# Pooled attention and a maxout layer on one core: weight casts as one-element reductions, a weight difference on GpSimd, another order of the first loads

## The chip, the cores and the metric

The kernel runs on one core of a Trainium2 chip. A core has five engines with a queue of their own each: TensorE (PE, matrix products; its weight loads are shown as PEld), VectorE (DVE), ScalarE (ACT), GpSimd (POOL) and SyncE (SP), which in this kernel only issues DMAs. Each engine takes its instructions strictly in the order of its queue and waits on semaphores for the others. The metric is the device time of one execution in microseconds (us); less is better.

## The reference

For 8 batches and 8 heads, with S = 1152 positions and head size D = 64, queries are averaged in pairs, attention is taken over all keys, and the result goes, all heads side by side, through a layer that takes the greater of two projections.

```
q_pool = q.reshape(B, H, S // 2, 2, D).mean(axis=3)          # 576 queries a head
attn   = softmax(q_pool @ k^T / sqrt(D))
x      = (attn @ v), heads side by side                      # 4608 tokens x 512
out    = maximum(x @ w1, x @ w2) @ w_out                     # 512 -> 1024 -> 512
```

All inputs and the output are float32 in HBM; the kernel works in bfloat16 with float32 accumulation.

## The kernel before

**The mathematics used.** maximum(h1, h2) is computed as relu(h1 - h2) + h2. So the kernel makes three things of the weights once, at the start: `wd` = w1 - w2 (bf16, 512 x 1024), `wo` = w_out in bf16, and `w21` = w2 @ w_out (512 x 512). A block of tokens then needs h = relu(x @ wd), and out = h @ wo + x @ w21.

**Weights.** Each of w1, w2 and w_out is loaded in four tiles of 512 KB (`w_load`, by part 0 = w2, 1 = w1, 2 = w_out, and tile 0 to 3). On landing, `w_cast` (L597) puts one VectorE instruction per tile in the queue: a copy to bf16 for w2 (L599, into `w2b`) and w_out (L606, into `wo`), a subtraction for w1 (L602, into `wd`). All are 128 partitions x 1024 elements, f32 in SBUF to bf16 in SBUF. `w2t_job` transposes w2 on TensorE (L614, copied out at L620), and when all tiles of w2 and w_out are cast, `w21_jobs` puts 32 products of 512 columns each (L630, copied out at L635) into TensorE's pool of filler work. These f32 tiles live in space that later holds other data: w2 in columns of `xT`, w1 where the hidden layer `gT` will be.

**Attention.** Two heads of a batch make a pair; there are 32, four to a batch. For each pair q, k and v come in one DMA of 576 KB each (`load_q`, `load_k`, `load_v`), into three buffers in turn. GpSimd makes bf16 of them: q with the sum of neighbours in two halves (`cast_q`, L319, 64 partitions x 576), k in L284, v in L326. For pairs 0 and 1 the sum for q is on VectorE (`cast_q0`, L310). q and k are transposed on TensorE for pairs 0 to 4 (L345, L361, L388, copied out by VectorE at L352, L368, L395) and by DMA after that (L302, L375). Scores (L510) are made in 324 groups of 512 columns for two heads into a ring of three PSUM buffers; ScalarE exponentiates each group (L517). A pair has 10.125 groups. The product with v (L420, and L432 for the last 64 rows) is divided by its sum on VectorE (`norm`: L442, L447, L452, into `xnat`). When the four pairs of a batch are done, its tokens are transposed into `xT` (L572 and L578 for the first and last batch, DMA for the others).

**Layer.** Blocks of 512 tokens: `h_pairs` (L699, copied out at L708) and `p_pair` (L732, copied out at L744), and, once all scores are issued, the single forms `h_jobs` (L672) and `p_job` (L767).

**Order of the work.** No order is written by hand except at the start. A planner (`class Plan`) runs while the program is built: it keeps an assumed time for each engine, with an assumed cost for each instruction, and the main loop picks at each step what TensorE does next: a group of scores, or one unit of a job (transposes, products with v, w21, layer). Jobs sit in two lanes, and more once the layer begins. Everything on the other engines is put in their queues as those picks bring it about. So an assumed cost changes the order of all that follows. `flush` runs ahead of each step; it hands DMAs from a list named `line` to SP, in the order of the list, when the assumed DMA backlog is under 4 us and the buffer is free; it emits the casts of a pair that has landed (`casts`); and it takes one weight cast from `lazy` when VectorE is assumed free and no transpose of q or k is near. The cast of the weights has no due time:

```
if lazy and plan.free.get("DVE", 0.0) <= now() and not any(
        queue[kind] and ready_at(queue[kind][0]) <= now() + 1.5 for kind in "qk") and all(
        j is None or j.kind not in "qk" for j in lane.values()):
    lazy.pop(0)()
```

**The start** (L1110 to L1150) is a list: q0 in two parts around k0, then loads that are issued at once (`load_q(1)`, `got_w((0, 0))`) and loads that go to `line` (`load('w', (0, 2), got_w, 'w2f2')`). `cast_v(0)` is put in GpSimd's queue there as well. In `got_w((part, tile))`, part and tile are as in `w_load`. Before the change the order is: q0 (first part), k0, q0 (rest), q1, k1, w2 tiles 0 and 1, v0, w2 tile 3; by `line` then w2 tile 2, q2, k2, w_out tiles 3, 1, 2, k3, v1, w_out tile 0, q3, w1 tiles 0 and 3, k4, w1 tile 2, v2, q4, w1 tile 1, v3. Later loads are appended to `line` as buffers come free.

**Who waits for wd.** `more_moe` opens a block of the hidden layer only when all tiles of `wd` are in the plan, and each unit of L699 names the tile `wd{ct}` that it reads.

Of the kernel before, what the change touches and what calls it, by code (L numbers as in the profile page):

```python
# [10 lines left out]
RELU = mybir.ActivationFunctionType.Relu  # L11
COPY = mybir.ActivationFunctionType.Copy
ALU = mybir.AluOpType


class Plan:
# [144 lines left out]
def bass_funnel_attn__then__act_maxout2_kernel(  # L161
# [10 lines left out]
    C, F = moe_w1.shape  # L172
# [21 lines left out]
    with ctx:  # L194
# [401 lines left out]

        def w_cast(part, ct):  # L597
            if part == 0:
                dve(lambda e: e.tensor_copy(w2b[:, ct, :], w2f[:, ct, :]),  # L599
                    [f"w2f{ct}"], [f"w2b{ct}"], 0.69)  # L600
            elif part == 1:
                dve(lambda e: e.tensor_tensor(  # L602
                    wd[:, ct, :], w1f[:, ct, :], w2f[:, ct, :], ALU.subtract),
                    [f"w1f{ct}", f"w2f{ct}"], [f"wd{ct}"], 1.4)
            else:
                dve(lambda e: e.tensor_copy(  # L606
                    wo[:, 2 * ct:2 * ct + 2, :], wof[:, 2 * ct:2 * ct + 2, :]),
                    [f"wof{ct}"], [f"wo{2 * ct}", f"wo{2 * ct + 1}"], 0.69)

        def w2t_job(ct):  # L610
            def go(e, m):
# [52 lines left out]
        def h_jobs(nb, tail):  # L664
            n0, n1 = hblocks[nb]
            size = n1 - n0
            g0 = n0 % RING
            jobs = []
            for ft in range(NF):
                def part(ct, ft=ft):  # L670
                    def go(e, m):
                        return e.matmul(fb[m][:, 0:size], wd[:, ct, ft * P:(ft + 1) * P],  # L672
                                        xT[:, ct, n0:n1], start=(ct == 0), stop=(ct == NC_ - 1))
                    return unit([f"wd{ct}"] + xkeys(n0, n1), 0.216 * size / 512, go)

# [12 lines left out]

        def h_pairs(nb):
            n0, n1 = hblocks[nb]  # L690
            size = n1 - n0
            g0 = n0 % RING
            jobs = []
            for f0 in range(0, NF, 2):
                def part(ct, turn, f0=f0):
                    def pair(e, m):
                        for k in range(2):
                            z = rows(turn ^ k)
                            last = e.matmul(  # L699
                                fb[m + k][:, 0:size], wd[z, ct, (f0 + k) * P:(f0 + k + 1) * P],  # L700
                                xT[z, ct, n0:n1], start=(turn == 0 and ct == 0),
                                stop=(turn == 1 and ct == NC_ - 1))
                        return last
                    return duo([f"wd{ct}"] + xkeys(n0, n1), 0.217 * size / 512, pair, turn == 1 and ct == 0)

                def evac(m, f0=f0):
                    w = [f"gT.{g}.{f0 + k}" for k in range(2) for g in gkeys(n0, n1)]
                    dve(lambda e: e.tensor_scalar_max(  # L708
                        gT[:, f0:f0 + 2, g0:g0 + size], wide[m // 2][:, :, 0:size], 0.0),
                        [f"f{m}", f"f{m + 1}"], w + [f"f{m}", f"f{m + 1}"], 0.16 + 2 * size / 960.0)  # L710
                jobs.append(Job("h", [part(ct, turn) for turn in range(2) for ct in range(NC_)],
                                evac, nb=nb, single=lambda f0=f0: h_jobs(nb, True)[f0:f0 + 2]))
            return jobs
# [114 lines left out]
        loaded = {}  # L828
        casts = []
        lazy = []  # L830
        todo = []
        MARGIN = 0.6
        K_PE = (0, 1, 2, 3, 4)
# [47 lines left out]
        def got_w(at):  # L881
            n, ct = at
            w_load(n, ct)

            def ready():
                w_cast(n, ct)
                if n == 0:
                    queue["w"].append(w2t_job(ct))
                w_done.add((n, ct))
                if n != 1 and all((m, c) in w_done for m in (0, 2) for c in range(NC_)):  # L890
                    queue["w"].extend(w21_jobs())
            later(f"{('w2f', 'w1f', 'wof')[n]}{ct}", lambda: lazy.append(ready))

        def enter(i):
            if i + 2 < NPAIR:
# [13 lines left out]
        def flush():  # L909
            for entry in list(todo):  # L910
                if plan.ops[entry[0]]["seen"] + entry[3] <= now():
                    todo.remove(entry)
                    entry[1]()
            while line and plan.dma_free - now() < DEPTH and plan.when("SP", w=[line[0][3]]) <= now() + 0.6:
                kind, i, fn, key = line.pop(0)
                fn(i)
                loaded[kind, i] = len(plan.ops) - 1
            for kind, i in list(casts):
                if not landed(kind, i):
                    continue  # L920
                if kind == "k":
                    force(("k", i - 2))
                    if k_hi.get(i - 2) != NT:
                        continue
                casts.remove((kind, i))
                {"k": start_k, "q": start_q, "v": start_v}[kind](i)
            if lazy and plan.free.get("DVE", 0.0) <= now() and not any(
                    queue[kind] and ready_at(queue[kind][0]) <= now() + 1.5 for kind in "qk") and all(
                    j is None or j.kind not in "qk" for j in lane.values()):
                lazy.pop(0)()  # L930
            for o in list(held):
                if plan.ops[plan.writer[f"osb{o}"]]["seen"] + 2.0 <= now():
# [32 lines left out]
        def more_moe():  # L965
            tail = nxt == NGR
            step = P if tail else 2 * P
            while h_at[0] < len(hblocks):
                n0, n1 = hblocks[h_at[0]]
                keys = xkeys(n0, n1) + [f"wd{ct}" for ct in range(NC_)]  # L970
# [149 lines left out]
        queue["k"].extend(ktrans_pe(0, K0))  # L1120
        whole = {"q": load_q, "k": load_k, "v": load_v}
        part = {"a": (0, "w2f"), "b": (2, "wof"), "c": (1, "w1f")}
        load_q(1)
        later('qraw1', lambda: (cast_q0(1,0,QU), queue['q'].append(qtrans0(1,0,QU))), margin=1.5)
        load_k(1)
        cast_k(1)
        queue['k'].extend(ktrans_pe(1))
        got_w((0, 0))
        got_w((0, 1))
        load_v(0)  # L1130
        cast_v(0)
        got_w((0, 3))
        load('w', (0, 2), got_w, 'w2f2')
        load('q', 2, load_q, 'qraw2')
        load('k', 2, load_k, 'kraw2')
        load('w', (2, 3), got_w, 'wof3')
        load('w', (2, 1), got_w, 'wof1')
        load('w', (2, 2), got_w, 'wof2')
        load('k', 3, load_k, 'kraw0')
        load('v', 1, load_v, 'vraw1')  # L1140
        load('w', (2, 0), got_w, 'wof0')
        load('q', 3, load_q, 'qraw0')
        load('w', (1, 0), got_w, 'w1f0')
        load('w', (1, 3), got_w, 'w1f3')
        load('k', 4, load_k, 'kraw1')
        load('w', (1, 2), got_w, 'w1f2')
        load('v', 2, load_v, 'vraw2')
        load('q', 4, load_q, 'qraw1')
        load('w', (1, 1), got_w, 'w1f1')
        load('v', 3, load_v, 'vraw0')  # L1150
# [120 lines left out]
```

## Time and profile before

| | before |
|---|---|
| median of five runs | 383.4 us (380.72, 383.66, 385.8, 383.4, 383.05) |
| the profiled execution | 380.73 us, of which the span from first to last instruction is 379.0 us |
| granted TensorE clock | 1.00 of full speed |
| busy: PE, ACT, POOL, DVE | 359.5, 316.3, 162.8, 144.9 us |
| HBM traffic | 62.91 MB read, 9.44 MB written |
| exponentials (L517) | x336, 305.3 us busy |
| scores (L510) | x1162, 119.7 us busy |

The page of the profile gives busy time by engine and by line, the same in 40 equal slices of the span, and the chain of work that ended last: from the last instruction back, at each step to what released it. A row of the timeline is: start, length, engine, line, operation, output and inputs with their shapes, how many, and in square brackets how long the engine stood idle before it and who released it. Busy TensorE time is modelled and says nothing on its own of how well the array is used; where TensorE stands idle, and for whom, is what is read here.

### The profile page before, as it was taken

The page shows a single profiled execution, that of the slowest core. Times are in us where ns is not written, and L with a number is a line of the kernel's source. Part 1 is how long each engine was busy: PE and PEld are TensorE (multiplying, and loading weights), DVE is VectorE, ACT ScalarE, POOL GpSimd, SP SyncE. Part 2 cuts the span into 40 slices and gives each one's busy share as a digit, 9 for nine tenths or more (in the row PEclk, how much of TensorE's full clock was granted, in tenths as well). Part 3 has the DMA queues.
Part 4 walks back from the last instruction along what each step waited for, and adds up shares of the span by engine and source line. Part 5 has one row for each costly group of instructions (what it writes and reads, how often), then busy time and mean ns, then how long its engine had stood idle before and what let it go on. Part 6 is the DMA issues. An engine that isn't in the chain of part 4 may idle for free.

```text
span 379.0 us, 12506 instructions
## 1 busy us (share of the span) xinstructions
PE 359.5 (95%) x5594; PEld 202.1 (53%) x5594; DVE 144.9 (38%) x304; ACT 316.3 (83%) x360; POOL 162.8 (43%) x133
## 2 busy tenths in 40 slices
PE   4889978999999999999999999998999999999996
PEld 1555545555555555554555555554655554665463
DVE  2766594442244313422442224421443145442231
ACT  4998889999999999999999999999899999811131
POOL 1356996676225750656246613654094601000000
PEclk9999999999999999999999999999999999999999
DMA  8999999999699999999799979999999974002324
GB/s 300 403 393 402 398 229 234 310 271 280 82 280 301 284 231 245 252 316 261 138 303 256 317 135 312 258 326 161 215 332 281 251 133 129 2 24 62 84 57 111
DMA packets 93542, 88.66 MB, mean 234 GB/s; under 512 B 66096, under 2 KB 66352, under 8 KB 93488
## 3 DMA queue, kind: packets, MB, share of 16 engines
q1 hardware_dynamic: 92608, 86.55, 88.4%
q10 hardware_dynamic: 880, 1.31, 0.9%
q8 instruction: 44, 0.72, 0.8%
q14 instruction: 10, 0.08, 0.1%
HBM read 62.91 MB, written 9.44 MB: 191 GB/s over the span
## 4 chain that ended last, share of the span: by engine, by line
PE 67%; ACT 25%; DVE 4%; DMA 1%; issue 1%; SPq 0%
ACT et L517 25%; PE sps L510 15%; PE fb L420 9%; PE fb L732 8%; PE sps L420 8%; PE sps L767 6%; PE sps L732 5%; PE sps L699 3%; PE sps L672 3%; DVE wd L602 2%; PE fb L699 2%; PE fb L432 2%; PE fb L630 2%; PE sps L432 1%; DMA kraw<-in_k_dram 1%
## 5 line engine op out<-in xcount | busy, mean ns | idle before, releaser
L517 ACT ACTIVATE et<-sps 128x1024 bf16<-128x1024 f32 (+1 forms) x336 | 305.3, 1020 | 18.8 <-PE sps L510 17.1
L510 PE MATMUL sps<-qpT,kT 64*128 64x256 bf16 (+7 forms) x1162 | 119.7, 289 | 5.0 <-ACT et L517 2.5
L319 POOL TENSOR_TENSOR qp<-qraw 64x576 bf16<-64x576 f32 x60 | 87.4, 1456 | 61.1 <-DMA qraw<-in_q_dram 58.6
L510 PEld LDWEIGHTS sps<-qpT,kT 64*128 64x128 bf16 x1162 | 38.6, 94 | 81.8 <-ACT et L517 66.1
L284 POOL TENSOR_SCALAR kbf<-kraw 128x1152 bf16<-128x1152 f32 x31 | 36.5, 1178 | 49.1 <-issue 15.5
L326 POOL TENSOR_SCALAR vE<-vraw 128x1152 bf16<-128x1152 f32 x32 | 37.8, 1182 | 40.3 <-DMA vraw<-in_v_dram 35.3
L420 PE MATMUL fb<-vE,et 128*128 128x65 bf16 x1368 | 48.3, 193 | 2.3 <-DVE xnat L452 2.3
L420 PEld LDWEIGHTS fb<-vE,et 128*128 128x128 bf16 x1368 | 43.5, 97 | 7.7 <-issue 4.2
L699 PE MATMUL sps<-xT,wd 64*128 64x512 bf16 (+1 forms) x240 | 35.9, 373 | 2.0 <-issue 1.4
L699 PE MATMUL fb<-xT,wd 64*128 64x512 bf16 x224 | 33.2, 376 | 0.1
L442 DVE RECIPROCAL rc<-fb 128x5 f32<-128x5 f32 (+1 forms) x38 | 7.1, 188 | 67.2 <-PE fb L420 67.2
L420 PE MATMUL sps<-vE,et 128*128 128x65 bf16 x936 | 32.8, 193 | 0.0
L732 PE MATMUL fb<-wo,stage 64*128 64x512 bf16 x224 | 32.1, 376 | 0.0
L420 PEld LDWEIGHTS sps<-vE,et 128*128 128x128 bf16 x936 | 29.7, 97 | 3.2 <-issue 2.5
L732 PE MATMUL sps<-wo,stage 64*128 64x512 bf16 x192 | 27.6, 376 | 0.0
L442 DVE RECIPROCAL rc<-sps 128x5 f32<-128x5 f32 (+1 forms) x26 | 4.9, 189 | 59.2 <-PE sps L420 59.2
L708 DVE TENSOR_SCALAR stage<-sps 128x1024 bf16<-128x1024 f32 (+1 forms) x15 | 18.1, 1205 | 19.4 <-PE sps L699 19.4
L708 DVE TENSOR_SCALAR stage<-fb 128x1024 bf16<-128x1024 f32 x14 | 17.1, 1223 | 19.9 <-PE fb L699 19.9
L767 PE MATMUL sps<-wo,stage 128*128 128x512 bf16 (+2 forms) x80 | 18.2, 358 | 0.0
L699 PEld LDWEIGHTS sps<-xT,wd 64*128 64x128 bf16 x240 | 11.2, 94 | 11.8 <-PE sps L699 1.5
L679 ACT ACTIVATE stage<-sps 128x256 bf16<-128x256 f32 (+2 forms) x12 | 4.5, 374 | 15.0 <-PE sps L672 13.7
L732 PE MATMUL fb<-w,xT 64*128 64x512 bf16 x112 | 16.6, 377 | 0.3
(70 smaller groups left out, 274.0 us busy)
## 6 DMA issues: line engine op xcount, KB each, us to landing
kraw<-in_k_dram SPq DMA_DIRECT2D x32, 576.0 KB, 7.4
vraw<-in_v_dram SPq DMA_DIRECT2D x32, 576.0 KB, 7.3
qraw<-in_q_dram SPq DMA_DIRECT2D x31, 576.0 KB, 6.8
out_dram<-stage SPq DMA_DIRECT2D x61, 128.0 KB, 2.5
xT<-in_moe_w_dram SPq DMA_DIRECT2D x4, 512.0 KB, 8.9
stage<-in_moe_w_out_dram SPq DMA_DIRECT2D x4, 512.0 KB, 14.6
stage<-in_moe_w_dram SPq DMA_DIRECT2D x4, 512.0 KB, 14.0
out_dram<-stage ACTq DMA_DIRECT2D x9, 128.0 KB, 2.6
```

Of the source, the lines that this page charges most:

```text
L284: op("POOL", lambda g: g.tensor_scalar(kbf[s][:, :, :, :].rearrange("p t h d -> p h t d"), kraw[r][:, :, :, :], 1.0, 1.0, ALU.mult, ALU.mu ...
L319: op("POOL", lambda g, half=half, a=a: g.tensor_tensor(qp[s][:, :, half, :], a[:, :, 0, :], a[:, :, 1, :], ALU.add), r=[f"qraw{r}"], w=[f" ...
L326: op("POOL", lambda g: g.tensor_scalar(vE[r][:, :, :, 0:D].rearrange("p t h d -> p h t d"), vraw[r][:, :, :, :], 1.0, 1.0, ALU.mult, ALU.m ...
L420: last = e.matmul(fb[m][:, sb * 66:sb * 66 + 65], et[:, a:a + P], vE[vs][:, t, half, 0:65], start=(t == 0), stop=(t == NT - 1))
L432: last = e.matmul(fb[m][rows(half), NCH * 66:NCH * 66 + 65], et[:, a:a + NB], vE[vs][:, t, half, 0:65], start=(t == 0), stop=(t == NT - 1))
L442: dve(lambda e: e.reciprocal(rc[half][:, 0:n], a[:, 0:n, 64:65]), [f"f{m}"], [f"rc{half}"], 0.19)
L510: last = e.matmul(sps[r][:, h, col:col + hi - lo], kT[i % 3][rows(h), t, :], qpT[i % 3][rows(h), lo:hi], start=True, stop=True)
L517: op("ACT", lambda e: e.activation(et2[:, :, c:c + z - a], sps[r][:, :, a - g * W:z - g * W], EXP, scale=scale), r=[f"s{r}"], w=keys + [f" ...
L699: last = e.matmul(fb[m + k][:, 0:size], wd[z, ct, (f0 + k) * P:(f0 + k + 1) * P], xT[z, ct, n0:n1], start=(turn == 0 and ct == 0), stop=(t ...
L708: dve(lambda e: e.tensor_scalar_max(gT[:, f0:f0 + 2, g0:g0 + size], wide[m // 2][:, :, 0:size], 0.0), [f"f{m}", f"f{m + 1}"], w + [f"f{m}" ...
L732: last = e.matmul(fb[m + k][:, :], lhs, rhs, start=(turn == 0 and j == 0), stop=(turn == 1 and j == NC_ + NF - 1))
L767: return e.matmul(fb[m][:, 0:c1 - c0], lhs, rhs[:, c0:c1], start=(j == 0), stop=(j == NC_ + NF - 1))
```

## The change

Three edits. First, the copies that make bf16 of w2 and w_out become a `tensor_reduce` with max over a last axis of length one, so that each output is the maximum of a single element; the planner's assumed cost goes from 0.69 to 1.13. Second, w1 - w2 goes from VectorE (one instruction of 1024 elements per tile) to GpSimd (`w_diff`, two instructions of 512 elements per tile), emitted by `flush` one at a time when GpSimd is assumed free; readers of `wd` name both halves. Third, the list of first loads has another order. Afterwards it is: q0 (first part), k0, q0 (rest), k1, w2 tile 1, q1, w_out tiles 1 and 3, v0; by `line` then w2 tiles 0 and 3, q2, k2, q3, k3, w2 tile 2, v1, w_out tile 2, q4, k4, w1 tile 3, v2, w_out tile 0, v3, w1 tiles 2, 1, 0.

```diff
         def w_cast(part, ct):
             if part == 0:
-                dve(lambda e: e.tensor_copy(w2b[:, ct, :], w2f[:, ct, :]),
-                    [f"w2f{ct}"], [f"w2b{ct}"], 0.69)
-            elif part == 1:
-                dve(lambda e: e.tensor_tensor(
-                    wd[:, ct, :], w1f[:, ct, :], w2f[:, ct, :], ALU.subtract),
-                    [f"w1f{ct}", f"w2f{ct}"], [f"wd{ct}"], 1.4)
+                dve(lambda e: e.tensor_reduce(
+                    w2b[:, ct, :], w2f[:, ct, :].unsqueeze(2), AX.X, ALU.max),
+                    [f"w2f{ct}"], [f"w2b{ct}"], 1.13)
             else:
-                dve(lambda e: e.tensor_copy(
-                    wo[:, 2 * ct:2 * ct + 2, :], wof[:, 2 * ct:2 * ct + 2, :]),
-                    [f"wof{ct}"], [f"wo{2 * ct}", f"wo{2 * ct + 1}"], 0.69)
+                dve(lambda e: e.tensor_reduce(
+                    wo[:, 2 * ct:2 * ct + 2, :], wof[:, 2 * ct:2 * ct + 2, :].unsqueeze(3), AX.X, ALU.max),
+                    [f"wof{ct}"], [f"wo{2 * ct}", f"wo{2 * ct + 1}"], 1.13)
+
+        def w_diff(ct, half):
+            f0, f1 = half * F // 2, (half + 1) * F // 2
+            op("POOL", lambda g: g.tensor_tensor(
+                wd[:, ct, f0:f1], w1f[:, ct, f0:f1], w2f[:, ct, f0:f1], ALU.subtract),
+                r=[f"w1f{ct}", f"w2f{ct}"], w=[f"wd{ct}.{half}"], cost=1.25)
...
-                    return unit([f"wd{ct}"] + xkeys(n0, n1), 0.216 * size / 512, go)
+                    return unit([f"wd{ct}.{half}" for half in range(2)] + xkeys(n0, n1), 0.216 * size / 512, go)
...
-            later(f"{('w2f', 'w1f', 'wof')[n]}{ct}", lambda: lazy.append(ready))
+            key = f"{('w2f', 'w1f', 'wof')[n]}{ct}"
+            if n == 1:
+                for half in range(2):
+                    later(key, lambda half=half: diffs.append((ct, half)))
+            else:
+                later(key, lambda: lazy.append(ready))
...
+            if diffs and plan.free.get("POOL", 0.0) <= now() + 0.3:
+                w_diff(*diffs.pop(0))
...
-        load_q(1)
-        later('qraw1', lambda: (cast_q0(1,0,QU), queue['q'].append(qtrans0(1,0,QU))), margin=1.5)
         load_k(1)
         cast_k(1)
         queue['k'].extend(ktrans_pe(1))
-        got_w((0, 0))
         got_w((0, 1))
+        load('w', (0, 0), got_w, 'w2f0')
+        load('w', (0, 3), got_w, 'w2f3')
+        load('q', 2, load_q, 'qraw2')
+        load_q(1)
+        later('qraw1', lambda: (cast_q0(1,0,QU), queue['q'].append(qtrans0(1,0,QU))), margin=1.5)
+        load('k', 2, load_k, 'kraw2')
+        got_w((2, 1))
+        load('q', 3, load_q, 'qraw0')
...
```

More of the change, by code (lines that the diff above doesn't have):

```diff
@@ L13 @@
 ALU = mybir.AluOpType
+AX = mybir.AxisListType
 class Plan:
@@ L703, in pair @@
                         return last
-                    return duo([f"wd{ct}"] + xkeys(n0, n1), 0.217 * size / 512, pair, turn == 1 and ct == 0)
+                    return duo([f"wd{ct}.{half}" for half in range(2)] + xkeys(n0, n1), 0.217 * size / 512, pair, turn == 1 and ct == 0)
                 def evac(m, f0=f0):
@@ L830, in bass_funnel_attn__then__act_maxout2_kernel @@
         lazy = []
+        diffs = []
         todo = []
@@ L969, in more_moe @@
                 n0, n1 = hblocks[h_at[0]]
-                keys = xkeys(n0, n1) + [f"wd{ct}" for ct in range(NC_)]
+                keys = xkeys(n0, n1) + [f"wd{ct}.{half}" for ct in range(NC_) for half in range(2)]
                 if n1 - RING > p_end[0] or any(key not in plan.writer for key in keys):
@@ L1127, in bass_funnel_attn__then__act_maxout2_kernel @@
         queue['k'].extend(ktrans_pe(1))
-        got_w((0, 0))
         got_w((0, 1))
+        load('w', (0, 0), got_w, 'w2f0')
[6 more added lines that the diff above has]
+        load('q', 3, load_q, 'qraw0')
+        load('k', 3, load_k, 'kraw0')
+        load('w', (0, 2), got_w, 'w2f2')
+        got_w((2, 3))
+        load('v', 1, load_v, 'vraw1')
+        load('w', (2, 2), got_w, 'wof2')
+        load('q', 4, load_q, 'qraw1')
+        load('k', 4, load_k, 'kraw1')
+        load('w', (1, 3), got_w, 'w1f3')
+        load('v', 2, load_v, 'vraw2')
+        load('w', (2, 0), got_w, 'wof0')
+        load('v', 3, load_v, 'vraw0')
+        load('w', (1, 2), got_w, 'w1f2')
         load_v(0)
         cast_v(0)
[L1132 to L1142, printed above, removed]
-        load('w', (1, 0), got_w, 'w1f0')
[L1144 to L1150, printed above, removed]
+        load('w', (1, 1), got_w, 'w1f1')
+        load('w', (1, 0), got_w, 'w1f0')
         rank = {"q": 6, "k": 6, "x": 5, "h": 5, "a": 4, "w": 3, "p": 1}
```

## The prediction

> **What bounds the kernel now.** I read four views in this order: the span in 40 slices, a table of stretches of the first 80 us, the chain of work that ended last between 20 and 66 us, and the timelines of TensorE and ScalarE there. Four rows of the slices, in tenths busy:
>
> ```profile
> PE   4889978999999999999999999998999999999996
> ...
> DVE  2766594442244313422442224421443145442231
> ACT  4998889999999999999999999999899999811131
> POOL 1356996676225750656246613654094601000000
> ```
>
> PE is at 9 nearly everywhere after the eighth slice (a slice is 9.5 us), at full clock in every slice: the matmul work is fixed, and what can be won is PE's idle time ahead of the moment from which it is saturated. The table says where that is (columns: stretch, its length, busy time of PE, PE's loads, DVE, ACT, POOL):
>
> ```profile
> 0.00:10.00 10.00, 4.27 (x43) 2.05 (x43) 2.33 (x7) 4.71 (x6) 2.38 (x11) 1.00 0.83 306
> 10.00:25.00 15.00, 13.57 (x231) 8.90 (x231) 10.78 (x21) 15.00 (x18) 6.24 (x5) 1.00 1.04 397
> 25.00:37.50 12.50, 10.79 (x167) 5.90 (x167) 8.62 (x16) 11.24 (x14) 7.56 (x6) 1.00 1.03 401
> 37.50:50.00 12.50, 12.00 (x191) 6.75 (x187) 7.97 (x14) 11.35 (x14) 11.79 (x9) 1.00 1.14 382
> 50.00:65.00 15.00, 11.61 (x246) 7.93 (x240) 9.89 (x20) 13.07 (x15) 11.60 (x8) 1.00 0.93 201
> ```
>
> PE idles 5.7, 1.4, 1.7, 0.5 and 3.4 us, 12.7 in all. The first 5.7 are the wait for the first data. The rest ends with the first hidden-layer matmul (L699) at 64.9 us, which needs batch 0's attention finished. Until then ScalarE's exponentials set the pace, and ScalarE's stalls move that moment:
>
> ```profile
> 8.32 26.89 ACT L517 ACTIVATE et<-sps 128x1024 bf16<-128x1024 f32 x30 [0.17 <-PE sps L510]
> 36.44 9.27 ACT L517 ACTIVATE et<-sps 128x1024 bf16<-128x1024 f32 x10 [1.23 <-PE sps L510]
> 46.83 8.56 ACT L517 ACTIVATE et<-sps 128x512 bf16<-128x512 f32 x10 [1.12 <-PE sps L510]
> 56.98 1.02 ACT L517 ACTIVATE et<-sps 128x1024 bf16<-128x1024 f32 x1 [1.59 <-PE sps L510]
> 58.34 8.36 ACT L517 ACTIVATE et<-sps 128x1024 bf16<-128x1024 f32 x9 [0.34 <-PE sps L510]
> ```
>
> Thirty groups run at 0.896 us each, then four stalls of 1.23 + 1.12 + 1.59 + 0.34 = 4.3 us, each waiting for PE. Why PE was late, the chain tells (start, length, what):
>
> ```profile
> 29.57 3.02 DVE wo L606 x3
> ...
> 44.67 1.94 DVE wd L602
> ...
> 48.21 6.03 DVE wd L602 x3
> 54.24 0.12 DVE rc L442
> ...
> 55.35 1.27 PE fb L420 x36
> ```
>
> Eleven us of weight casts lie on it. Nobody needs them then; the normalisations (L442 to L452) stand behind them in VectorE's queue, and PE waits for the bank those release: 2.27 us at 55.35.
>
> **The weight casts (L599, L606).** The trace has the durations of the old forms, and of GpSimd's nearest (least, median and greatest ns, then first and last start):
>
> ```profile
> L599 DVE CAST xT<-xT x4: 683/685/1902, 14.4 to 17.8; 128x1024 bf16<-128x1024 f32 x4
> L606 DVE CAST wo<-stage x4: 681/1160/1904, 25.5 to 30.7; 128x1024 bf16<-128x1024 f32 x4
> L602 DVE TENSOR_TENSOR wd<-stage,xT x4: 1676/2090/2426, 44.6 to 51.8; 128x1024 bf16<-128x1024 f32 x4
> L319 POOL TENSOR_TENSOR qp<-qraw x60: 1393/1400/2369, 17.3 to 298.6; 64x576 bf16<-64x576 f32 x60
> ```
>
> A cast is 0.68 us alone and up to 1.90 beside GpSimd work; the eight took 3.8 + 4.7 = 8.5. No row shows a tensor_reduce. Nearest is L708, which takes 128x1024 f32 one element at a time out of PSUM in 1.22 us; L635 does 512 in 0.69, so 1.04 ns an element. Ends: 1.07 us (1024 elements, no fixed cost) and 2.4 (twice L708, if every one-element group costs a second step). I take 1.2, L708's: 8 x 1.2 = 9.6, that is 1.1 more than the 8.5.
>
> A rule speaks against it: the Trainium skill, VectorE: DVE Perf Modes, Rules for kernel authors, calls tensor_reduce the slowest operation there, to be expected at one element per cycle. By it and the uncontended row the sum is 8 x (1.2 - 0.68) = +4.2 us. But the row's casts were not uncontended. The skill's page SBUF — State Buffer, Who interferes with whom, says a cast in the two-port mode and a GpSimd instruction lock each other out, a tensor_reduce on trn2 never does, and a two-input VectorE operation collides with GpSimd reads. The row agrees on the first and third: 1.90 against 0.68, and L602 at 2.09 where L708's size takes 1.22. That the reduce is free of it no trace here shows; I go with it, hence +1.1 and not +4.2. Its cover is VectorE's slack: 21.7 us busy in the first 37.5. Without cover it costs at most its 1.1.
>
> **w1 minus w2 to GpSimd (L602).** VectorE loses 8.1 us, 8.0 of them on the chain. GpSimd gains eight halves. Nearest row: L319, 1.40 us for 576 elements of two f32 inputs, so 512 take 1.25 and eight take 10.0. L319 uses 64 partitions; ends are 1.1 (the skill's page GPSIMD Engine Reference, 3.1 Elementwise, has 4497 ns for 2048 elements: an estimate of 4497/4) and 2.5, if 128 partitions took twice L319. I take 1.25. That page's 4.1 Engine selection sends elementwise work to VectorE, since GpSimd is some two times slower: 10.0 against four times 1.22, so a loss of 5 us by the rule. By the trace it costs VectorE's queue 8.1, and GpSimd gets back its own stretching: in the first 100 us 22 x (1554-1400) + 11 x (1228-1150) + 11 x (1240-1150) ns = 5.2 us. GpSimd nets +4.8. Cover: w1's last tile lands at about 41 us and the difference is first read at some 60. TensorE now waits for two halves per tile, with no more reached than before. Behind a half in GpSimd's queue stand the q, k and v casts, each late by up to 1.25; pair 5's are the tight ones, since their transposes land 6 us after issue and ScalarE reaches pair 5 at 53 us (8.32 + 50 x 0.896).
>
> **The new order of loads.** As many DMAs on SP's queue as before, none added on another; at 400 GB/s 576 KB take 1.47 us and 512 KB 1.31. Counting what stands ahead: q1 is passed by k1 and a weight tile, +2.8 (from 7.8, which is 1.47 before k1's landing at 9.23, to 10.6); v0, q2 and k2 +1.3 each (13.3 to 14.6; 17.3 to 18.6); q3 -6.9 (30.2 to 23.3), q4 -8.2, and the last w_out tile +7.2 (28.7 to 35.9). Queues passed: SP's alone; on GpSimd the v0 cast still precedes that of q2.
> Late loads: q1's cast began at 10.05 for a score at 13.9 that ScalarE wanted at 16.4 (8.32 + 9 x 0.896): covered by 2.5 us. k2: its cast ended at 22.2, its transpose began at 24.2: covered. v0: its first use is at 17.97: covered.
> Early loads: q3's cast ran 30.17 to 33.85, and the transposes at 34.88 and the scores at 36.0 waited for it: that 1.23 us stall goes.
> The late w_out tile: w21 (L630) needs all casts. They ended at 32.6; now 35.9 + 1.2 = 37.1. PE did 11 of w21's 32 matmuls, 2.9 us, before 37.5; that filler goes. In its place come pair 4's transposes (1.3) and scores ScalarE no longer stalls (0.5), so PE idles about 1.1 more there. It is work put off, not added.
>
> **The sum.** If all ScalarE stalls go, the first hidden-layer matmul moves from 64.9 to 60.6. Does the work fit? From 37.5 PE had 12.0 + 11.6 = 23.6 us; plus 2.9 - 1.8 put off, less the scores of 4.3 us (4.8 groups x 0.37 = 1.8): 22.9 in 23.1 us. Just. So 4.3 is the upper end, or 5.7 if the 1.4 of PE's idle time from 10 to 25 us went as well. The other way: idle after 37.5 falls from 3.9 to 0.5 (latencies such as 0.41 at 57.35 stay), idle before rises by 1.1: 2.3 gained, the lower end. The stall is what the earlier q3 and the emptied VectorE queue act on, so I take a value near the 4.3: **3.9 us**. The profiled execution took 380.7 (span 379.0 and 1.7 around it), so 376.8; that execution lies 2.7 below the median of five, 383.4, and against the median I say **379.5**.
>
> **Rivals.** *The gain is taken back by GpSimd*: it was 11.8 us busy in the 12.5 before 50; six halves (7.5) from w1's last three tiles meet pair 5's casts there, and those come 2 to 3 us late. For: the POOL row's 99 there. Against: pair 4's q cast moves out to 30 us and the stretching ends. Gain 1.2: 382.2.
> *The front starves (slower)*: ScalarE loses pair 1's q and pair 2's k. It decides once q1's lateness in VectorE's queue exceeds 2.5 us. At full price 2.8 + 1.3 and w21's 2.9 unreplaced is +7.0; only the 2.3 of waits behind L602 still go: 388.1. For: three loads are later, and k2's copy ended at 25.54 for a group due at 26. Against: the slack counted above.
> *The reduce takes 2.4 us (slower)*: eight times 1.2 more, in a queue where evacuations wait: 379.5 + 9.6 = 389.1. Deciding point: 1.7 us each, where the 3.9 is gone. Nothing here shows the operation.
>
> **How the numbers follow.** Forecast 0.56 with its own range of 377.7 to 381.1 (gains 5.7 to 2.3); some 0.40 of it beyond 1% and 0.16 within. GpSimd takes it back 0.14; starved front 0.18; slow reduce 0.12. One per cent, 3.8 us, is about what a measurement of this kernel tells from no change: five runs spread by 1.3%. So faster 0.40, same 0.30 (0.16 and 0.14), slower 0.30 (0.18 and 0.12). Range: 376.0 to 388.0; the low end lets the idle time fall by the 7 us that follow the first data, the high end stops short of the slow reduce.
>
> **What would show it.** Right: tensor_reduce near 1.2 us with one value, no maximum at 1.9; halves near 1.25 on POOL; POOL casts back at 1.40 and 1.15; no L602 in the chain; the 2.27 and 1.23 waits gone; the first L699 near 61 us; PE idle in 25 to 37.5 up to some 2.8. Wrong: reduces over 1.7; halves over 1.9; ScalarE idle near 16 or 26 us; transposes of pair 5 landing after 53; a first L699 at 64 or later.

## The result, and the profile after

The change makes the kernel slightly faster. The median is 380.5 us over 22 runs (378.83 to 385.31) against 383.46 us over 41 runs of the kernel before. The ratio is 0.994, 95% interval 0.9919 to 0.996, which is 0.6% or 2.3 us. It leaves out slow executions, those over 1.5% above the fastest of their kernel; the plain medians lie 3.0 us apart. The forecast was 379.5, with 3.9 us gained.

The profiled execution after took 379.87 us (span 378.1), close to its median. The profiled execution before took 380.73 us, 2.7 below its median. So this pair of traces shows 0.9 us of difference, and not all of the 2.3 need be in it. The two differ in TensorE's granted clock as well: 1.00 throughout in the front before, and at half for 3.4 us in the front after.

Busy shares in 40 slices of the kernel after, to be laid beside the same rows of before:

```profile
DVE  2767344423234115413442315422433135342231
ACT  4999978999999999999999999999999999811131
POOL 1277999478127751566255705573094601000000
```

In the front, VectorE's 5 9 4 4 4 2 2 4 4 (from the fifth slice) has become 3 4 4 4 2 3 2 3 4: the block of subtractions in the sixth slice is gone. GpSimd has 9 9 9 (fifth to seventh slice) where it had 9 9 6. The stretches (length, busy PE, its loads, DVE, ACT, POOL, then granted clock, DMA share, GB/s):

```profile
0.00:10.00 10.00, 4.27 (x43) 2.04 (x43) 2.44 (x7) 4.72 (x6) 1.77 (x11) 1.00 0.79 279
10.00:25.00 15.00, 12.51 (x214) 8.03 (x214) 11.65 (x20) 14.91 (x18) 6.11 (x6) 1.00 1.04 404
25.00:37.50 12.50, 10.89 (x191) 7.71 (x191) 7.60 (x16) 11.79 (x15) 10.04 (x9) 0.86 1.04 398
37.50:50.00 12.50, 12.50 (x202) 6.99 (x199) 4.60 (x10) 12.47 (x15) 12.33 (x11) 1.00 1.00 385
50.00:65.00 15.00, 14.35 (x243) 8.83 (x241) 6.88 (x20) 12.13 (x14) 14.67 (x13) 1.00 1.16 237
```

Length less busy PE gives idle times of 5.7, 2.5, 1.6, 0 and 0.65 us, 10.5 together, against 12.8 before: 2.3 less (unrounded: 12.76 and 10.48). After 37.5 us the idle time fell from 3.9 to 0.65; from 10 to 25 it rose by 1.1.

Not all of the 2.3 is work done earlier, because a matmul at half clock counts as busy for longer. Over half-microsecond stretches, busy time multiplied by the granted clock comes to 52.9 us up to 65 us after the change, and to 52.2 before, where the clock was full. By this estimate from the two traces the front is ahead by 0.7 us, close to the 0.9 of the whole execution.

ScalarE's timeline, with its idle time and the releaser in brackets:

```profile
8.31 17.71 ACT L518 ACTIVATE et<-sps 128x1024 bf16<-128x1024 f32 x19 [0.16 <-PE sps L511]
26.61 28.20 ACT L518 ACTIVATE et<-sps 128x256 bf16<-128x256 f32 x32 [0.58 <-PE sps L511]
57.20 3.77 ACT L518 ACTIVATE et<-sps 128x1024 bf16<-128x1024 f32 x4 [2.39 <-PE sps L511]
61.45 9.47 ACT L518 ACTIVATE et<-sps 128x1024 bf16<-128x1024 f32 x11 [0.47 <-PE sps L511]
```

Thirty-two groups run without a stall where two stalls stood before, but one new stall of 2.39 us comes at 54.8. The chain of work that ended last says why (start, length, what):

```profile
53.70 1.08 PE fb L634 x5
...
55.69 0.70 DVE w L639
...
57.20 1.03 ACT et L518
```

L634 is w21, the product of the weights that was put off with the late w_out tile. It stands ahead of the scores that ScalarE waits for. No weight cast and no subtraction is left in this part of the chain.

The three new rows, as least, median and greatest ns, with first and last start:

```profile
L600 DVE TENSOR_REDUCE xT<-xT x4: 1209/1210/1212, 13.3 to 30.9; 128x1024 bf16<-128x1024 f32 x4
L604 DVE TENSOR_REDUCE wo<-stage x4: 1208/1208/1210, 16.2 to 38.0; 128x1024 bf16<-128x1024 f32 x4
L610 POOL TENSOR_TENSOR wd<-stage,xT x8: 1267/1274/1276, 37.6 to 56.6; 128x512 bf16<-128x512 f32 x8
```

A reduce takes 1.21 us, also the one at 31.99 us, beside which GpSimd's q sum ran from 32.25 us on. A half takes 1.27.

Behind the front the changed kernel first loses time and then gains some: from 80 to 160 us PE idled 2.3 us, against 0.6 before, and from 240 to 300 us 0.4 against 1.5, at full clock in both. The two largest waits of the first of these stretches, in PE's timeline:

```profile
98.83 0.39 PE L511 MATMUL sps<-qpT,kT 64*128 64x192 bf16 x4 [0.53 <-ACT et L518]
...
144.55 0.61 PE L703 MATMUL fb<-xT,wd 64*128 64x512 bf16 x4 [0.74 <-issue]
```

### The profile page after: what moved, and what is told of

It reads as the page before. It is cut to its first block, busy times and chain, and to the rows that moved or that the text cites. A ratio compares the mean times of both kernels' runs of the same rounds, so it can differ in the third digit from the quotient of the medians.

```text
span 378.1 us, 12511 instructions
## 1 busy us (share of the span) xinstructions
PE 360.1 (95%) x5594; PEld 202.4 (54%) x5594; DVE 138.2 (37%) x300; ACT 316.4 (84%) x360; POOL 167.4 (44%) x141
## 4 chain that ended last, share of the span: by engine, by line
PE 65%; ACT 24%; DMA 5%; SPq 2%; issue 1%; POOL 1%; DVE 0%; POOLq 0%
ACT et L518 24%; PE sps L511 15%; PE sps L421 10%; PE fb L421 9%; PE sps L736 8%; PE sps L771 6%; DMA kraw<-in_k_dram 5%; PE fb L736 3%; PE fb L703 2%; PE fb L634 2%; PE sps L676 2%; PE sps L433 2%; PE fb L676 2%; PE fb L433 1%; PE sps L703 1%; SPq L593 1%
## 5 line engine op out<-in xcount | busy, mean ns | idle before, releaser
L421 PE MATMUL fb<-vE,et 128*128 128x65 bf16 x1152 | 41.0, 193 | 0.0
L421 PE MATMUL sps<-vE,et 128*128 128x65 bf16 x1152 | 40.4, 193 | 0.0
L421 PEld LDWEIGHTS sps<-vE,et 128*128 128x128 bf16 x1152 | 36.5, 97 | 4.1 <-issue 3.5
L703 PE MATMUL fb<-xT,wd 64*128 64x512 bf16 (+1 forms) x240 | 35.5, 373 | 0.9 <-issue 0.7
L703 PE MATMUL sps<-xT,wd 64*128 64x512 bf16 x224 | 33.3, 376 | 0.1
L712 DVE TENSOR_SCALAR stage<-sps 128x1024 bf16<-128x1024 f32 x14 | 17.1, 1224 | 21.1 <-PE sps L703 21.1
L712 DVE TENSOR_SCALAR stage<-fb 128x1024 bf16<-128x1024 f32 (+1 forms) x15 | 18.1, 1205 | 18.3 <-PE fb L703 18.3
L736 PE MATMUL sps<-w,xT 64*128 64x512 bf16 x112 | 16.6, 377 | 0.2
L703 PEld LDWEIGHTS fb<-xT,wd 64*128 64x128 bf16 x240 | 11.2, 94 | 9.7 <-issue 1.2
L771 PE MATMUL sps<-wo,stage 128*128 128x512 bf16 (+2 forms) x72 | 15.8, 355 | 0.0
L736 PEld LDWEIGHTS sps<-wo,stage 64*128 64x128 bf16 x224 | 10.7, 94 | 8.3 <-issue 0.4
## 6 DMA issues: line engine op xcount, KB each, us to landing
stage<-in_moe_w_out_dram SPq DMA_DIRECT2D x4, 512.0 KB, 12.5
```

The costliest lines, as they stand in the source:

```text
L421: last = e.matmul(fb[m][:, sb * 66:sb * 66 + 65], et[:, a:a + P], vE[vs][:, t, half, 0:65], start=(t == 0), stop=(t == NT - 1))
L703: last = e.matmul(fb[m + k][:, 0:size], wd[z, ct, (f0 + k) * P:(f0 + k + 1) * P], xT[z, ct, n0:n1], start=(turn == 0 and ct == 0), stop=(t ...
L712: dve(lambda e: e.tensor_scalar_max(gT[:, f0:f0 + 2, g0:g0 + size], wide[m // 2][:, :, 0:size], 0.0), [f"f{m}", f"f{m + 1}"], w + [f"f{m}" ...
L736: last = e.matmul(fb[m + k][:, :], lhs, rhs, start=(turn == 0 and j == 0), stop=(turn == 1 and j == NC_ + NF - 1))
L771: return e.matmul(fb[m][:, 0:c1 - c0], lhs, rhs[:, c0:c1], start=(j == 0), stop=(j == NC_ + NF - 1))
```

## The experiments

Ratios are to the kernel before, measured next to each run, with 95% intervals. Runs 1 to 4, 5 to 8 and 9 to 12 were measured on three different chips, where the kernel before had medians of 382.96, 383.22 and 383.65 us; so kernels of different groups are compared by ratio. Nine of the twelve profiles took longer than the median of their kernel, so they show where time can go and not the usual execution.

The theories have letters in the expectations. A is the prediction's: VectorE's queue, freed of subtractions, carries the gain. B: the collision of VectorE's copies with GpSimd was the cost (called the port there). C: the new order of loads carries it; in it, the early q3 and k3 do (E), or the late w1 tiles (F). And, beside all of these: the planner, given other assumed costs, writes other queues, so that a part's effect is that of another plan and not of the part.

**1. The reduce alone, in identical queues.** The kernel before, with the reduce at the copies' old assumed cost: the order of every queue stays, and eight VectorE instructions differ.

```
-dve(lambda e: e.tensor_copy(w2b[:, ct, :], w2f[:, ct, :]), ..., 0.69)
+dve(lambda e: e.tensor_reduce(w2b[:, ct, :], w2f[:, ct, :].unsqueeze(2), AX.X, ALU.max), ..., 0.69)
```
(and the same for w_out)

> The kernel before with the eight weight casts as one-element tensor_reduce and nothing else: the planner keeps its old assumed cost, so all five queues hold the same instructions in the same order as before, and only eight VectorE instructions differ. Theory A (the cost was VectorE's queue, mainly the four subtractions L602): casts take 1.2 us each with one value, the GpSimd operations beside them fall back to 1.40 and 1.15, but L602 keeps its 2.1 us and its place, so the first hidden-layer matmul stays at 64 to 65 us and the time within 0.5 us of before. Rival B (the port was the cost, so freeing GpSimd is what pays): most of the 2.3 us comes here, first hidden-layer matmul near 62 us.

Measured: 382.47 us, ratio 0.9977 (0.9956 to 0.9997). That is 0.9 us, with an interval that almost touches no change. In the groups of its first 70 us the mean of GpSimd's q sums falls from 1642 to 1463 ns, and the four subtractions still take 2158 ns each. The cast no longer collides with GpSimd; the two-input subtraction still does.

**2. The subtraction on GpSimd alone.** Old copies, old order, new `w_diff` and the readers of both halves.

```
-dve(lambda e: e.tensor_tensor(wd[:, ct, :], w1f[:, ct, :], w2f[:, ct, :], ALU.subtract), ..., 1.4)
+op("POOL", lambda g: g.tensor_tensor(wd[:, ct, f0:f1], w1f[:, ct, f0:f1], w2f[:, ct, f0:f1], ALU.subtract), ..., cost=1.25)
```

> The kernel before with w1 - w2 on GpSimd in halves and nothing else (old copies, old order of loads). Theory A: the 8 us of L602 leave VectorE's queue, the 2.27 us wait of PE goes, first hidden-layer matmul near 62 us, time 2 us (0.5%) under before. Rival B (the port): copies still collide with GpSimd, up to 1.9 us each, and GpSimd has 10 us more, so no gain, or 1 us lost. Rival C (the order of the loads carries the gain): no gain.

Measured: 384.23 us, ratio 1.0029 (1.0006 to 1.0053), slower by a little. Two rows of its timelines, VectorE's and ScalarE's:

```profile
29.98 4.31 DVE L603 CAST wo<-stage 128x1024 bf16<-128x1024 f32 x3
...
38.14 9.27 ACT L518 ACTIVATE et<-sps 128x1024 bf16<-128x1024 f32 x10 [2.04 <-PE sps L511]
```

Three w_out copies take 4.31 us, 1.44 each where one alone takes 0.68, and ScalarE stalls for 2.04 soon after. That the copies cause the stall is not shown: this profile took 386.93 us, the longest of the run's 22, and TensorE was at half clock from 28.5 to 32 us. Taking the 8 us of subtractions out of VectorE's queue is no gain by itself.

**3. The new order alone.** The kernel before with the changed list of first loads, and nothing else.

> The kernel before with the new order of first loads and nothing else. Theory A: the ScalarE stall at 36 us goes with the earlier q3, but w1's tiles land later, so the subtractions sit at 45 to 55 us in VectorE's queue and still hold the normalisations: first hidden-layer matmul at 63.5 to 65, time within 1 us of before. Rival C: the order carries the gain, 2 us or more, first hidden-layer matmul near 62.

Measured: 380.61 us, ratio 0.9931 (0.9904 to 0.9959): as much as the whole change. The subtractions are still on VectorE. ScalarE stalls for 5.2 us between 16 and 65 us here, more than the 4.3 of before. VectorE's timeline:

```profile
39.11 1.22 DVE L602 TENSOR_TENSOR wd<-stage,xT 128x1024 bf16<-128x1024 f32 x1
42.61 2.13 DVE L602 TENSOR_TENSOR wd<-stage,xT 128x1024 bf16<-128x1024 f32 x1
...
47.62 1.56 DVE L602 TENSOR_TENSOR wd<-stage,xT 128x1024 bf16<-128x1024 f32 x1
```

All four (one is left out) stand singly, with other work between them, where before three stood in a row for 6.03 us with the normalisations behind them.

**4. Both engine edits, old order.** The changed kernel with the list of loads put back.

> The changed kernel with the old order of first loads. Theory A: as good as the whole change or up to 1 us better, since w21's weights come as early as before (filler from 33 us) and VectorE's queue is free: first hidden-layer matmul at 61 to 62, time 2 to 3 us under before. Rival C: without the order no gain, first hidden-layer matmul at 64 or later.

Measured: 383.03 us, ratio 1.0015 (0.9995 to 1.0036). PE's idle time to 65 us is 12.55, near that of before, and in this profile TensorE was at half clock twice, for 3.4 us each; ScalarE still stalls by 1.90 and 1.62 us. With run 3 this settles the main question: the order carries the gain, and the two engine edits together bring nothing without it.

**5. The changed kernel with copies.** `tensor_copy` in place of `tensor_reduce` at the assumed cost of 1.13, in queues identical to the changed kernel's.

> The changed kernel with its eight tensor_reduce put back to tensor_copy, the planner's assumed cost left at 1.13, so that all queues hold the same instructions in the same order and only eight VectorE instructions differ. If the reduce is what keeps GpSimd free: the copies take 0.68 to 1.9 us, qp and wd halves beside them stretch up to 2.2 us, and the time is 0.5 to 1 us over the changed kernel. If the port doesn't matter in this order: equal to the changed kernel within 0.3 us.

Measured: 381.81 us, ratio 0.9959 (0.9938 to 0.9981). The reduce is worth some 0.19% in this plan (0.9959 to 0.994; the intervals overlap), as it was 0.23% in the plan of run 1. The copies' rows, busy and mean ns:

```profile
L603 DVE CAST wo<-stage 128x1024 bf16<-128x1024 f32 x4 | 4.3, 1101 | 0.0
...
L600 DVE CAST xT<-xT 128x1024 bf16<-128x1024 f32 x4 | 3.6, 927 | 0.0
```

Eight copies took 7.9 us and eight reduces take 9.7. The form that is busy for longer was not the slower one in either plan.

**6. Order and reduce, subtraction on VectorE.** The changed kernel with whole-tile subtractions back on VectorE.

```
+elif part == 1:
+    dve(lambda e: e.tensor_tensor(wd[:, ct, :], w1f[:, ct, :], w2f[:, ct, :], ALU.subtract), ..., 1.4)
...
```

> The changed kernel with w1 - w2 back on VectorE as one instruction of 1024 per tile (new order and tensor_reduce stay). The runs so far: order alone 0.9931, reduce alone in the old plan 0.9977, difference on GpSimd alone 1.0029. If the three add up, this is the best of the kernels, 0.991 or 3.5 us under before. If the difference on GpSimd is needed once the casts take 1.2 us on VectorE (theory A): the subtractions collide with normalisations again, first hidden-layer matmul at 64 or later, and it is slower than the changed kernel by 1 us or more.

Measured: 381.68 us, ratio 0.9964 (0.9939 to 0.999), not to be told from the changed kernel (0.994). In the new order, then, where the subtraction runs makes no difference that these intervals show. Neither expectation came true: the three parts do not add up, and the first hidden-layer matmul is at 62.7 us, not at 64 or later.

**7. Which loads? q3 and k3 early.** The kernel before, with q3 and k3 ahead of the w_out tiles (q4 falls behind w1 tiles 0 and 3, ahead of k4).

```
 load('k', 2, load_k, 'kraw2')
+load('q', 3, load_q, 'qraw0')
+load('k', 3, load_k, 'kraw0')
 load('w', (2, 3), got_w, 'wof3')
...
```

> The kernel before, in whose list only q3 and k3 are moved ahead of the w_out tiles (and what they passed comes later by as much); the first eight loads, all casts and the subtraction are as before. Theory E (the order pays because the attention inputs come early): ScalarE's stall at 36 us goes, TensorE is fed from 30 us on, 1.5 to 2.5 us under before, first hidden-layer matmul near 62. Theory F (it pays because w1's tiles land late and one by one, so that no three subtractions stand together ahead of a normalisation): in this plan, too, each subtraction stands alone in VectorE's queue, so it gains as well; the next run tells them apart.

Measured: 380.18 us, ratio 0.9922 (0.9896 to 0.9948): the whole gain, in VectorE's and GpSimd's old split of the work. What theory E said of the front did not come: the stall at 36 us is gone, but one of 3.51 us stands at 45.6, and the first hidden-layer matmul is at 65.1.

**8. w1 late.** The kernel before, with only w1's four tiles moved to the end of the list.

> The kernel before, in whose list only w1's four tiles are moved to the end; q3 keeps its place behind nine weight tiles, q4, k4, v2 and v3 move up. In VectorE's queue the subtractions then stand as two, one and one and no longer as one and three. Theory F: the 2.27 us wait of TensorE for a normalisation goes and so does ScalarE's stall of 1.59 at 57 us: 1.5 us or more under before. Theory E: ScalarE's stall of 1.23 at 36 us stays and with it the time: within 0.7 us of before.

Measured: 382.09 us, ratio 0.9981 (0.9957 to 1.0005), and 12.63 us of idle PE to 65 us. Theory F falls as the carrier in this kernel.

**9. q3 alone.** The smallest edit:

```
 load('k', 2, load_k, 'kraw2')
+load('q', 3, load_q, 'qraw0')
 load('w', (2, 3), got_w, 'wof3')
 ...
 load('w', (2, 0), got_w, 'wof0')
-load('q', 3, load_q, 'qraw0')
```

> The kernel before, in whose list only q3 is moved ahead of the w_out tiles; k3 keeps its place behind three of them and lands 1.5 us later than before. Theory E in its narrow form (q3's late cast, which the transposes at 34.9 us and ScalarE's stall at 36 us waited for, was the cost): most of the gain, 1.5 us or more under before. If both tensors are needed, or if it is the separate subtractions (here one, two, one in VectorE's queue): within 0.7 us of before.

Measured: 380.15 us, ratio 0.991 (0.9877 to 0.9944). One load moved ahead of four weight tiles, k3 and v1 is worth as much as the whole change. ScalarE in this kernel:

```profile
8.28 36.38 ACT L517 ACTIVATE et<-sps 128x1024 bf16<-128x1024 f32 x40 [0.16 <-PE sps L510]
46.61 9.48 ACT L517 ACTIVATE et<-sps 128x512 bf16<-128x512 f32 x11 [1.96 <-PE sps L510]
```

Forty groups without a stall, where before the thirty-first waited 1.23 us for q3's transposes. The next stall, of 1.12 us before, is 1.96 here, and 0.98 and 0.48 follow: 3.4 us in all against 4.3. So the gain is shown, and that this one stall carries it is not.

**10 and 11. The engine edits on top of early q3 and k3.** Run 7 with the reduce at the old assumed cost (identical queues), and run 7 with the reduce and the subtraction on GpSimd.

> The kernel with only q3 and k3 moved up, plus the eight casts as tensor_reduce with the old assumed cost: the same instructions in the same order in all queues as with q3 and k3 moved up alone, eight VectorE instructions apart. If the reduce is worth what it was in the old plan (0.9977 of it) and in the changed kernel (copies there 0.9959, reduces 0.994), both are free of each other and this is the best: 0.990, or 379.5 us. If it only pays where copies collide: there the four w_out casts took 2.8 us together, nearly uncollided, and would take 4.8, so it is equal or up to 1 us slower than q3 and k3 moved up alone.

Measured: 380.54 us, ratio 0.9915 (0.9889 to 0.9941), against 0.9922 without the reduce: nothing that can be told.

> The changed kernel with the other order: the old one with only q3 and k3 moved up. Theory E with the difference on GpSimd as a cost (alone 1.0029; with the reduce in the old order 1.0015): slower than q3 and k3 moved up alone by 1 us or more, 381 to 382. If the difference on GpSimd only cost where q3 came late: equal to it or better, 379.5 to 380.

Measured: 384.49 us, ratio 1.0007 (0.9977 to 1.0037). The intervals of 10 and 11 are apart: in this order, the subtraction on GpSimd (with the assumed cost of 1.13, and the plan that follows) takes the whole gain away. Its profiled front does not show where: PE idles 10.85 us to 65, at full clock, much as in run 10. The w1 tiles stand early in this list, so the halves come ahead of later q and k casts in GpSimd's queue; that this is the cause was not tested.

**12. The changed kernel with q3 and k3 late.** If E holds inside the changed kernel too, moving both back behind w2 tile 2, v1 and w_out tile 2, some 4 us, should lose the gain.

```
-load('q', 3, load_q, 'qraw0')
-load('k', 3, load_k, 'kraw0')
 load('w', (0, 2), got_w, 'w2f2')
 got_w((2, 3))
 load('v', 1, load_v, 'vraw1')
 load('w', (2, 2), got_w, 'wof2')
+load('k', 3, load_k, 'kraw0')
+load('q', 3, load_q, 'qraw0')
```

> The changed kernel, in whose list q3 and k3 are moved back behind w2's tile 2, v1 and w_out's tile 2, so that they land about 4 us later (near 28 us); the casts, the difference on GpSimd and the rest of the order stay. Theory E (the early q3 and k3 carry the gain): the gain goes, 383 us or more, ScalarE stalls again between 30 and 50 us. Rival: the rest of the new order carries it (weights in another sequence, w1 last): equal to the changed kernel within 0.7 us.

Measured: 379.51 us, ratio 0.9882 (0.9851 to 0.9913), the lowest ratio of all, from six executions, and its interval lies just below that of the change. So E is sufficient in the old kernel and not what carries the gain in the changed one. q3's transposed copy begins at 34.8 us there, hardly before the 35.35 of the kernel before, yet ScalarE does not stall for it:

```profile
17.25 37.17 ACT L518 ACTIVATE et<-sps 128x1024 bf16<-128x1024 f32 x42 [0.57 <-PE sps L511]
56.53 12.22 ACT L518 ACTIVATE et<-sps 128x1024 bf16<-128x1024 f32 x14 [2.11 <-PE sps L511]
```

Where its lead over the change lies is open. The stretch from 80 to 120 us, of the changed kernel and then of this one (columns as above):

```profile
80.00:120.00 40.00, 38.95 (x652) 21.00 (x647) 13.79 (x30) 38.05 (x42) 20.93 (x17) 1.00 0.98 228
```

```profile
80.00:120.00 40.00, 39.76 (x666) 21.56 (x663) 13.60 (x29) 38.23 (x43) 19.75 (x16) 1.00 0.97 223
```

To 160 us PE idles 0.5 us in it and 2.3 in the changed kernel; these 1.8 us are near the difference of the ratios (0.0058 of 383, 2.2 us). But this profile took 382.17 us, the longest of its six and longer than the changed kernel's 379.87: from 240 to 300 us PE idles 2.2 us in it and is at half clock for 3.4, against 0.4 and none. This is one profile of each, and no further run tested it.

**The granted clock in all of them.** TensorE runs at half clock in episodes, and in the profiles each one before the last few microseconds lasts 3.4 us or twice that. One of 3.4 us takes 1.7 us of 380 off the mean clock, which is then 0.995; each execution's mean was recorded. Executions counted as none (0.998 and more), one (0.994 to 0.996), and two or more (0.991 and less):

| kernel | ratio | none | one | two or more |
|---|---|---|---|---|
| before, as measured next to runs 1 to 12 | 1 | 12 | 91 | 53 |
| the change | 0.994 | 14 | 8 | 0 |
| 1: reduce | 0.9977 | 4 | 10 | 8 |
| 2: subtraction on GpSimd | 1.0029 | 4 | 13 | 5 |
| 3: order | 0.9931 | 11 | 3 | 0 |
| 4: both, old order | 1.0015 | 5 | 9 | 8 |
| 5: change with copies | 0.9959 | 14 | 8 | 0 |
| 6: order and reduce | 0.9964 | 12 | 2 | 0 |
| 7: early q3, k3 | 0.9922 | 9 | 9 | 4 |
| 8: late w1 | 0.9981 | 14 | 8 | 0 |
| 9: early q3 | 0.991 | 2 | 6 | 1 |
| 10: 7 and reduce | 0.9915 | 1 | 5 | 0 |
| 11: 10 and subtraction on GpSimd | 1.0007 | 3 | 5 | 6 |
| 12: change, late q3, k3 | 0.9882 | 5 | 1 | 0 |

The kernel before has a median of 381.0 us without an episode, 383.0 with one and 384.8 with two or more; the changed kernel 380.1 and 380.8. So with no episode on either side the change is worth 0.9 us, as in the pair of profiles. Among executions without one, run 3's order shows no gain: 380.7 in 11, against 380.5 in the four of the kernel before measured next to it, though four are few. Two or more are found in 5 of 115 executions of the kernels with a ratio under 0.997 and in 80 of 236 of before and runs 1, 2, 4 and 11. Run 8 is the exception, with none and hardly a gain. Where episodes can fall, run 1's profile shows, in the queues of the kernel before (two of its stretches, with the granted clock third from the end; at 386.07 us it is the longest of its 22):

```profile
25.00:37.50 12.50, 11.16 (x154) 6.69 (x153) 7.86 (x15) 10.66 (x13) 6.91 (x6) 0.73 1.03 400
50.00:65.00 15.00, 12.05 (x209) 8.07 (x210) 10.77 (x16) 11.57 (x14) 11.47 (x7) 0.89 0.76 162
```

Thus a good part of the median gain goes together with fewer episodes. Whether fewer episodes are its cause was not tested: no run changes them alone.

## Why the prediction was right and wrong

**The reduce, 1.2 us with one value: right**, 1.21. The forecast weighed a rule that speaks against the operation with one that says it never locks with GpSimd (the Trainium skill, SBUF — State Buffer, Who interferes with whom). The traces now side with the second: 56 reduces in seven kernels took 1.207 to 1.212 us, where copies in the same queue places averaged 0.93 and 1.10. That it costs no time was right too: in three identical-queue pairs (runs 1, 5 and 10) it is 0.9 us or less to the good, and clear of no change in the first alone.

**The halves, 1.25 us: right**, 1.27. That GpSimd gets its stretching back is right too; the page's row for the q sums:

```profile
L320 POOL TENSOR_TENSOR qp<-qraw 64x576 bf16<-64x576 f32 x60 | 84.0, 1400 | 57.8 <-DMA qraw<-in_q_dram 55.5
```

Its mean is now the 1400 ns that was the median.

**The waits of 2.27 and 1.23 us: gone, and L602 off the chain: right.** But "the emptied VectorE queue" was named as what the stalls act on, and **that step failed**. Run 2 empties that queue of subtractions and is slower; run 4 also makes the casts free of GpSimd and is not faster; run 3 leaves the subtractions on VectorE and has the whole gain. That L602 stood on the chain was a matter of the plan, three in a row at 48.2 us, and not of the engine. The other half of that sentence, the earlier q3, was the better one: run 9 shows that it suffices in the old kernel. The prediction named both and could not tell their shares, having read a chain in which each wait has one releaser.

**The size: in range, by luck in part.** The ScalarE stalls were taken to go wholly (4.3 us). They measured 0.58 + 2.39 + 0.47 = 3.4 us afterwards, so 0.9 went. The 2.39 is w21: "work put off, not added" was right, but the forecast let it fill gaps, and it fell where ScalarE needed scores. The step itself fails, and not only its size: between the first data and 65 us, run 3 has 5.2 us of stalls with the whole gain, and run 11 has 3.5 with none. The other reading, PE's idle time, said 2.3 for the front. It measured 2.3, which equals the median gain, but this is a coincidence: in full-clock work the front is 0.7 us ahead, and the pair of profiles ends 0.9 apart. What the sum leaves out is the half clock. It took "full clock in every slice" from one profile, and 12 of 156 executions of the kernel before are without an episode. The median gain goes beyond 0.9 only in executions that have one.

**The first hidden-layer matmul near 61 us: right** at 61.9 (64.9 before), but it is no measure of the end. It came 3.0 us earlier, and the end in that pair of profiles 0.9. Run 7 has it at 65.1 us with the full gain, run 4 at 68.8 with none. The premise that the end follows that moment is wrong. That the planner mixes the remaining front work in later is a likely reason, not a tested one.

**Covered loads: nearly.** k2 was called covered, and ScalarE stalled 0.58 us at 26.0 for its scores. v0's cast began at 16.7 us, where its load was expected at 14.6. In the profiles of runs 3, 5, 6 and 12, whose first nine loads are the same, it began at 14.5 to 15.8: the first loads shift by some 2 us between executions.

**The rivals.** The reduce did not take 2.4 us and the front did not starve. GpSimd taking the gain back came nearest of them in the number (382.2) and wasn't the mechanism in the changed kernel: run 6, with the subtraction on VectorE, is no faster.

**What stays open.** Which piece of the new list carries the gain inside the changed kernel, since neither early q3 and k3 (run 12) nor late w1 in the old kernel (run 8) does it. Why the subtraction on GpSimd costs 0.9% in run 11, where 11 of 14 executions have a half-clock episode. Why the new order has fewer of them. And a spot near 265 us, where hidden-layer matmuls wait for a batch's token transposes: PE idles 0.4 us from 240 to 300 in the profile after and 1.5 in that before, but up to 3.6 in others, as PE's waits from 80 to 340 us in run 9 show (waiting, released by, total, count, longest):

```profile
PE sps L699 <- DMA xT<-xnat: 3.3, 1, 3.3
```

That profile took 383.83 us, the longest of its nine, and TensorE is at half clock for 3.4 us after this wait. So this spot varies, and some of the median gain that the pair of profiles does not show may lie there.

## What to carry to other kernels

Where a planner orders the queues, a changed cost or load re-plans everything: judge an operation in identical queues, and an order by itself, before crediting either. An operation on the chain is not yet a cause; look for the plan that put it in front of others, and try the smallest move (here one load ahead of the weight tiles) before moving work to another engine. Before reading a gain from a pair of profiles, compare their granted clock and weigh busy time by it: neither ScalarE's stalls nor TensorE's idle time in the front ranks these kernels (10.9 us of idle time in run 7 with the whole gain, and in run 11 with none). And see how often each kernel's executions show the clock of the profile that is read.

## What the runs showed of the hardware

The granted TensorE clock fell to half for about 3.4 us in the changed kernel's front (12.5 us at 0.86 in its table of stretches are 3.5 us at half). Two stretches of its trace:

```profile
27.00:29.00 2.00, 1.11 (x15) 0.92 (x17) 0.00 (x0) 1.98 (x3) 1.91 (x2) 0.68 1.04 401
29.00:31.00 2.00, 2.00 (x19) 1.05 (x17) 1.36 (x4) 2.00 (x3) 1.24 (x2) 0.50 1.04 401
```

The Trainium skill (TensorE: Matmul & The Clock Gate, Part 1) gives half clock after an idle window of about 3.4 us. Here PE was sparse and not idle, 1.11 us busy of 2. Over the nine profiles with such episodes, PE was busy for 0.7 to 2.2 of the 3.4 us ahead of each. That is not enough to bring one about: the profile before has 1.13 us busy from 52.0 to 55.4 us and stays at full clock. Executions with one episode are 0.7 us longer than those without in the changed kernel (medians of 380.8 and 380.1 us), and 2.0 us in the kernel before (383.0 and 381.0).

A two-input VectorE operation of 1024 elements took 1.22 us with GpSimd idle and 2.13 at the next place, beside a GpSimd q sum (run 3); three copies took 4.31 us beside GpSimd; the reduce, with the same number of elements, did not move by more than 4 ns in the changed kernel. And GpSimd's cost followed the elements per partition: 2.43 ns each on 64 partitions (1400/576) and 2.49 on 128 (1274/512).
